# The expert stage in a written order on all engines, with two reordered edges, in a float32 chain of attention, experts and a dense layer

## The chip, the cores and the metric

The kernel runs on one core of a Trainium2 chip. The metric is the device time of one execution in microseconds, lower is better; the time given is the median of several executions. TensorE multiplies, VectorE, ScalarE and GpSimd do elementwise work on tiles of 128 partitions, SyncE's queue issues most of the transfers from DRAM.

## The reference, cut to what matters

Three layers follow each other, all in float32.

```python
# attention: q, k, v [4, 8, 576, 64], s [4, 8, 576]
scores = q @ k^T / sqrt(64)
cum = np.cumsum(np.maximum(s, 0.0), axis=-1)
scores = where(causal, -1e9, scores + minimum(-(cum_q - cum_k), 0.0))
x = softmax(scores) @ v                # then [2304, 512]
# experts: 8 of them, one for each token
logits = normalize(x) @ normalize(expert_emb).T / tau
e = argmax(logits);  gate = softmax(logits)[e]
x = gate * (relu(x @ w1[e]) @ w2[e])   # w1 [512, 1024], w2 [1024, 512]
# dense
h = x @ w_in                           # [512, 2048]
out = (h * np.cos(h)) @ w_out          # [2048, 512]
```

## The kernel before

**Order.** `moe_kernel` (line 43) calls the stages. Up to and with `steps.late()` everything stands under a manual schedule of all engines: what an engine does follows the order of the program. `finish()` (most of the expert stage) and `moe2` (the dense stage) stand under a manual schedule of SyncE alone: there a planner puts the instructions of the other engines in an order, by costs and due times of its own.

**Attention** (line 105). 16 pairs of heads, four steps each; step n of pair p has scores `sco` (lines 310 and 316, products of 64 rows), `mx` (line 336, VectorE: adds the decay, takes the maximum), `ex` (ScalarE, exponential), `tr` (transposes, line 352) and the products with v. The decay of a pair lies in `c_t`, which `load_c` reads back from DRAM (`cumd`, written from ScalarE's queue on line 198). For the first pair `first_c` makes it on TensorE instead (line 208), as a product of a selector with the 32 rows of `cum`. `mask` adds the causal part, `setup_a` to `setup_d` prepare the router and are put at points of the loop by `at`.

**Experts** (line 745). A step (r, f) is eighth f of the hidden layer of expert r; r = -1 stands for the first tokens of one expert, taken early, and r = 0 for its rest; 72 steps in all, n = 8 (r + 1) + f. A step has a weight tile [128, 1024] that `weights` loads into one of three `raw` buffers and that `split` (line 95) parts in two: `wh` (ScalarE, line 99) and its rest `wl` (VectorE, line 101). `emit_h` makes 12 products, the relu `hh` on ScalarE (964) and its rest `hl` on VectorE (965); `emit_o` makes 12 products into four accumulators (992 to 994), one step later. After the last eighth of an expert the accumulators go to `x2h` (ScalarE, 999) and `x2l` (VectorE, 1000), at a place that is read from memory into a register by `offset` (817), for ScalarE and VectorE. `windows` (822) is a chain of small operations for the overflow loop, and `token_numbers` (1007) scatters row numbers by GpSimd, 20 times; both are tied to an instruction behind which the planner may put them. `load_x` and `xt_parts` load and transpose an expert's tokens.

**Dense** (line 1244). 80 steps, each a pair of one of 16 chunks of weights and one of five blocks of tokens (one of 256, four of 512): `emit_h` 12 products (1287 to 1289) and then h·cos h (`h_cos_h`, 1145: ScalarE, VectorE, ScalarE with Sin, VectorE), `gh` (ScalarE, 1294) and `gl` (VectorE, 1295); `emit_o`, two steps behind, 12 products (1307 to 1309). The chunks lie in DRAM as pairs of 32-bit words (float64) and are converted in halves by `load_chunk` (1213) with `to_f32_parts` (1131): lines 1136, 1137, 1140, 1141, 1230 and 1231 on VectorE, 1228 on ScalarE. `start_chunk` puts a chunk's generator into `g.tasks`, and `advance` takes every task one part further. Chunks 0 to 3 are started in the last expert steps, 4 and 5 at the head of the dense stage, and a chunk's conversion is finished in one go where a step needs it:

```python
            for _ in g.loading.pop(c, ()):
                pass
            wh, wl = ring[c]
```

Of the kernel before, what the change touches and what calls it, by code (L numbers as in the profile page):

```python
# [7 lines left out]
F32 = mybir.dt.float32  # L8
# [15 lines left out]
E, F = 8, 1024  # L24
# [18 lines left out]
def moe_kernel(ctx, tc, qd, kd, vd, sd, ied, embt, tau, ident, maskd, trid, wcat, wf, out):  # L43
# [9 lines left out]
    g.chunks, g.tasks, g.loading = {}, [], {}  # L53
# [11 lines left out]
    with ExitStack() as m1:  # L65
        with tc.manual_schedule(engines={ET.SP, ET.PE, ET.Activation, ET.DVE, ET.Pool}):
            attention(g, wcat, qd, kd, vd, sd, ied, embt, tau, ident, maskd, trid)
            steps, finish = moe1(g, m1, wcat, wf)
# [36 lines left out]
def attention(g, wcat, qd, kd, vd, sd, ied, embt, tau, ident, maskd, trid):  # L105
# [6 lines left out]
    with ExitStack() as st:  # L112
# [49 lines left out]
        def mask(p):  # L162
# [21 lines left out]

        s_t = sx.tile([128, S], F32, tag="sx", name="s_t")[0:B * H]
# [15 lines left out]
        sel2 = one.tile([B * H, 128], F32, name="sel2")  # L201
        nc.vector.tensor_copy(out=sel2.rearrange("p (a b) -> p a b", a=2), in_=idt[0:B * H, 0:2].unsqueeze(2).to_broadcast([B * H, 2, 64]))
# [11 lines left out]
        load(1)  # L214
# [6 lines left out]
        emb_t = one.tile([128, 4, E], F32, name="emb_t")  # L221
# [5 lines left out]
        ones_f = one.tile([128, 128], F32, name="ones_f")  # L227
# [15 lines left out]
        nc.gpsimd.memset(ones_f, 1.0)  # L243
# [7 lines left out]
        def setup_loads():  # L251
            nc.sync.dma_start(out=ie, in_=ied)
            nc.sync.dma_start(out=emb_t, in_=embt)
# [21 lines left out]
        def setup_a():  # L275
            nc.gpsimd.tensor_copy(out=tri_b, in_=tri_f)
            nc.gpsimd.tensor_tensor(out=sq, in0=emb_t, in1=emb_t, op=ALU.mult)
# [347 lines left out]
        at(1, "b", setup_b)  # L625
        at(2, "rb", setup_c)
        at(2, "b", setup_d)
# [40 lines left out]
        mx(2)  # L668
        ex(2)
        next(mask(1))  # L670
        mx(3)
        fills = [0, 1, 2, 3, 4, 4, 5, 5]
        for p in range(NPAIR):
# [23 lines left out]
            tr(n)  # L697
# [47 lines left out]
def moe1(g, st, wcat, wf):  # L745
# [3 lines left out]
    if True:  # L749
# [66 lines left out]
        def offset(r):  # L816
            if r < 0:
                return 0
# [3 lines left out]
        def windows():  # L822
# [7 lines left out]
            nc.vector.tensor_tensor(out=over[:, 0:1], in0=over[:, 0:1], in1=g.pf[:, 2:3], op=ALU.add)  # L830
            nc.vector.tensor_tensor(out=over, in0=pick[:, 2, :], in1=over, op=ALU.subtract)
            wi = sm.tile([128, NWIN], I32, name="wi")
            nc.gpsimd.iota(wi, pattern=[[1, NWIN]], base=0, channel_multiplier=0)
            wn = sm.tile([128, NWIN], F32, name="wn")
            nc.vector.tensor_copy(out=wn, in_=wi)
            wn128 = sm.tile([128, NWIN], F32, name="wn128")
            nc.vector.tensor_scalar(out=wn128, in0=wn, scalar1=128.0, scalar2=None, op0=ALU.mult)
            s5 = [128, E, NWIN]
            gt = sm.tile(s5, F32, name="gt")
            nc.vector.tensor_tensor(out=gt, in0=bc(over, 2, s5), in1=bc(wn128, 1, s5), op=ALU.is_gt)  # L840
            trips = sm.tile([128, E], F32, name="trips")
            nc.vector.tensor_reduce(out=trips, in_=gt, axis=AX.X, op=ALU.add)
            nc.vector.tensor_tensor(out=tmp, in0=bc(g.ef, 2, s3), in1=bc(g.ef, 1, s3), op=ALU.is_gt)
            nc.vector.tensor_tensor(out=tmp, in0=tmp, in1=bc(trips, 1, s3), op=ALU.mult)
# [99 lines left out]
        def emit_h(n):  # L944
# [22 lines left out]
            if n == 17:  # L967
                with tc.issue_after(ins.ins):
                    windows()
# [423 lines left out]
```

## Time and profile before

| | |
|---|---|
| median of 3 executions | 834.78 us (833.91 to 834.93) |
| profiled execution | 834.91 us |
| its span | 833.0 us (1.9 us lie around it) |
| busy TensorE / VectorE / ScalarE / GpSimd | 802.2 / 569.6 / 421.9 / 139.0 us |
| mean granted clock of TensorE | 0.992 |
| start of the first product, of the last | 4.70 us, 821.31 us |
| start of the last scatter to DRAM | 823.28 us |

The profile is one execution, with times from the start of its span. PE is TensorE, PEld its weight loads, DVE VectorE, ACT ScalarE, POOL GpSimd, SP SyncE; a name with a q at its end is an engine's queue. Attention lasts to about 160 us, the experts from there to 412, the dense stage to the end. An idle time in brackets stands before the instruction of its row, with what ended it.

### The profile page before, as it was taken

The numbers are of one execution on the slowest core, as the hardware profiler recorded it, in microseconds if no ns is written. First come the engines' busy times: TensorE is split into PE (matmuls) and PEld (weight loads), VectorE is DVE, ScalarE is ACT, GpSimd is POOL, SyncE is SP. The second block draws the span as 40 slices with busy tenths as digits, with TensorE's granted clock in tenths as the row PEclk, the third lists the DMA queues.
The fourth block names the chain that finished last, engine by engine and source line by source line (L and its number), as shares of the span: only waits on it lengthen the run. The fifth ranks groups of instructions, "written<-read, shape, count | busy, mean of one in ns | idle before, by whom it ended". The sixth has DMA issues, their size and how long they took to land. (4 is left out here: it accounts for less than half of the span.)

```text
span 833.0 us, 15110 instructions
## 1 busy us (share of the span) xinstructions
PE 802.2 (96%) x5607; PEld 666.0 (80%) x5607; DVE 569.6 (68%) x1254; ACT 421.9 (51%) x894; POOL 139.0 (17%) x274
## 2 busy tenths in 40 slices
PE   7999999999999999999989999999999999999994
PEld 4666666689999999999868888888888888888883
DVE  5879897974765565566989577775877758444462
ACT  4988888732545454555255453333433434333331
POOL 4447665340011101100000000000000000000133
PEclk9999999999999999999989999999999999999998
DMA  7999875548757689774432111110111100000122
GB/s 239 311 354 349 260 242 168 171 162 323 260 152 190 141 161 194 205 174 164 142 101 77 51 51 50 52 52 1 50 52 51 51 1 2 1 0 1 52 78 102
DMA packets 41712, 109.06 MB, mean 131 GB/s; under 512 B 7392, under 2 KB 7904, under 8 KB 41632
## 3 DMA queue, kind: packets, MB, share of 16 engines
q1 hardware_dynamic: 38032, 98.50, 39.9%
q0 software_dynamic: 3552, 9.45, 3.1%
q8 instruction: 46, 0.75, 0.4%
q14 instruction: 34, 0.28, 0.1%
q10 hardware_dynamic: 48, 0.07, 0.0%
HBM read 92.19 MB, written 15.81 MB: 130 GB/s over the span
## 5 line engine op out<-in xcount | busy, mean ns | idle before, releaser
L101 DVE TENSOR_TENSOR wl<-wraw,wh 128x1024 fp32r<-128x1024 f32 x64 | 78.2, 1224 | 66.9 <-ACT wh L99 66.8
L1287 PE MATMUL h_ps<-x2h,wh 128*128 128x512 f32 (+1 forms) x320 | 118.9, 371 | 1.1 <-DVE x2l L1000 1.1
L1307 PE MATMUL facc<-wh,gh 128*128 128x512 f32 x288 | 115.7, 402 | 3.8 <-ACT gh L1294 3.8
L1288 PE MATMUL h_ps<-x2l,wh 128*128 128x512 f32 (+1 forms) x320 | 118.4, 370 | 0.0
L1289 PE MATMUL h_ps<-x2h,wl 128*128 128x512 f32 (+1 forms) x320 | 118.3, 370 | 0.0
L1309 PE MATMUL facc<-wh,gl 128*128 128x512 f32 x288 | 114.8, 399 | 0.0
L1308 PE MATMUL facc<-wl,gh 128*128 128x512 f32 x288 | 114.7, 398 | 0.0
L1148 ACT ACTIVATE ki<-h_ps 128x512 int32<-128x512 f32 (+1 forms) x80 | 44.5, 557 | 119.9 <-PE h_ps L1289 119.4
L1149 DVE SCALAR_TENSOR_TENSOR ki<-ki,h_ps 128x512 f32<-128x512 int32 (+1 forms) x80 | 50.5, 632 | 71.4 <-ACT ki L1148 71.0
L99 ACT CAST wh<-wraw 128x1024 fp32r<-128x1024 f32 x64 | 67.1, 1050 | 52.6 <-PE acc L993 47.5
L1319 POOL DMA_INDIRECT out_dram<-oacc,ti x18 | 17.5, 971 | 439.9 <-DVE oacc L1317 436.2
L604 ACT ACTIVATE s_sb<-s_sb,mx 128x576 f32<-128x576 f32 (+2 forms) x144 | 83.0, 581 | 5.5 <-DVE mx L336 5.4
L1150 ACT ACTIVATE ki<-ki,hpi 128x512 f32<-128x512 f32 (+1 forms) x80 | 54.5, 682 | 48.3 <-DVE ki L1149 48.3
L993 PE MATMUL acc<-hl,wh 128*128 128x256 f32 (+7 forms) x256 | 76.6, 299 | 0.7 <-DVE hl L965 0.7
L992 PE MATMUL acc<-hh,wh 128*128 128x256 f32 (+7 forms) x256 | 77.3, 302 | 0.0
L994 PE MATMUL acc<-hh,wl 128*128 128x256 f32 (+7 forms) x256 | 76.4, 298 | 0.0
L1294 ACT CAST gh<-ki 128x512 fp32r<-128x512 f32 (+1 forms) x80 | 46.3, 578 | 53.1 <-DVE ki L1151 53.1
L1287 PEld LDWEIGHTS h_ps<-x2h,wh 128*128 128x128 f32 x320 | 60.1, 188 | 13.4 <-DVE x2l L1000 1.3
L1288 PEld LDWEIGHTS h_ps<-x2l,wh 128*128 128x128 f32 x320 | 60.2, 188 | 12.3 <-DVE x2l L1000 0.6
L1151 DVE TENSOR_TENSOR ki<-h_ps,ki 128x512 f32<-128x512 f32 (+1 forms) x80 | 50.7, 634 | 27.3 <-ACT ki L1150 27.3
L1289 PEld LDWEIGHTS h_ps<-x2h,wl 128*128 128x128 f32 x320 | 60.2, 188 | 11.3
L959 PE MATMUL h_ps<-xth,wh 128*128 128x368 f32 (+6 forms) x224 | 68.6, 306 | 0.0
(241 smaller groups left out, 1686.6 us busy)
## 6 DMA issues: line engine op xcount, KB each, us to landing
wraw<-in_wcat_dram SPq DMA_DIRECT2D x64, 512.0 KB, 4.8
wraw<-in_wf_dram SPq DMA_DIRECT2D x32, 512.0 KB, 3.7
k_t<-in_kd_dram SPq DMA_DIRECT2D x16, 496.0 KB, 9.8
c_t<-cumd SPq DMA_DIRECT2D x15, 512.0 KB, 6.9
xr<-zr SPq DMA_DIRECT2D x8, 768.0 KB, 9.4
xw<-xr SPq DMA_DIRECT2D x7, 768.0 KB, 8.3
q_t<-in_qd_dram SPq DMA_DIRECT2D x16, 320.0 KB, 6.6
v_t<-in_vd_dram SPq DMA_DIRECT2D x16, 320.0 KB, 7.8
```

The lines of the kernel that those rows point to most:

```text
L101: nc.vector.tensor_tensor(out=lo, in0=raw, in1=hi.bitcast(F32), op=ALU.subtract)
L604: nc.scalar.activation(**kw)
L959: nc.tensor.matmul(out=ps[:, 0:c], lhsT=wh[:, sl], rhs=th[:, k, 0:c], start=(k == 0), stop=False)
L992: nc.tensor.matmul(out=ps[:, 0:c], lhsT=wh[:, sl], rhs=hh[:, 0:c], start=(f == 0), stop=False)
L993: nc.tensor.matmul(out=ps[:, 0:c], lhsT=wh[:, sl], rhs=hl[:, 0:c], start=False, stop=False)
L994: nc.tensor.matmul(out=ps[:, 0:c], lhsT=wl[:, sl], rhs=hh[:, 0:c], start=False, stop=(f == 7))
L1287: nc.tensor.matmul(out=ps[:, 0:w], lhsT=wh[:, sl], rhs=g.x2h[:, k, a0:a1], start=(k == 0), stop=False)
L1288: nc.tensor.matmul(out=ps[:, 0:w], lhsT=wh[:, sl], rhs=g.x2l[:, k, a0:a1], start=False, stop=False)
L1289: nc.tensor.matmul(out=ps[:, 0:w], lhsT=wl[:, sl], rhs=g.x2h[:, k, a0:a1], start=False, stop=(k == 3))
L1307: nc.tensor.matmul(out=acc[t], lhsT=gh[:, sl], rhs=wh[:, 512:1024], start=(c == s), stop=False)
L1308: nc.tensor.matmul(out=acc[t], lhsT=gh[:, sl], rhs=wl[:, 512:1024], start=False, stop=False)
L1309: nc.tensor.matmul(out=acc[t], lhsT=gl[:, sl], rhs=wh[:, 512:1024], start=False, stop=(c == e))
```

## The change

Four things are edited. (1) At the start a memset of ones comes first on GpSimd and nine products of ones first on TensorE; a dummy Exp comes early on ScalarE; the selectors and `cum` get 128 partitions (the rest zero); `cumd` is written from SyncE's queue; loads change order; one of `mask`'s additions goes to GpSimd; `mx(0)`, `sco(2)`, `tr(0)`, the square of the embeddings and `setup_b` to `setup_d` come earlier. (2) `finish` and a new `last_steps` stand under the manual schedule of all engines. A table `when` says behind which step a weight tile is split, and the load three tiles ahead is issued behind it; the place register of an expert is loaded in its step f = 4; `windows` becomes a generator of which three operations follow at a time; `token_numbers` stands in program order without its statement that the scatters are independent. (3) Of the chunks only 0, and the first part of 1, is converted before the expert stage ends; chunks 2 to 5 start in dense steps 1, 4, 8 and 11; a step asks for the half it needs (`half_of`); the first part in the dense stage is put behind the last `x2l`; a dummy Sin stands in `overlap` behind `gate_b`. (4) In the last four dense steps all h come before the last o, pairs of blocks share a tile, and the second products go by token tile.

```diff
@@ moe_kernel @@
             steps.late()
-        with tc.manual_schedule(engines={ET.SP}):
             finish()
+            last_steps()
@@ attention @@
-                    nc.vector.tensor_tensor(out=c[:, h, 512:640], in0=c[:, h, 512:640], in1=mk_f[:, 0:128], op=ALU.add)
+                    (nc.gpsimd if h else nc.vector).tensor_tensor(out=c[:, h, 512:640], in0=c[:, h, 512:640], in1=mk_f[:, 0:128], op=ALU.add)
...
+        ones_f = one.tile([128, 128], F32, name="ones_f")
+        nc.gpsimd.memset(ones_f, 1.0)
...
+        nc.sync.dma_start(out=mk_f, in_=maskd)
         load(0)
-        nc.sync.dma_start(out=mk_f, in_=maskd)
+        emb_t = one.tile([128, 4, E], F32, name="emb_t")
+        nc.sync.dma_start(out=emb_t, in_=embt)
+        w_ps = bank("w_ps")
+        for _ in range(9):
+            nc.tensor.matmul(out=w_ps[:, 0:128], lhsT=ones_f, rhs=ones_f, start=True, stop=True)
+        nc.scalar.activation(out=one.tile([128, 1], F32, name="exp0"), in_=ones_f[:, 0:1], func=ACTF.Exp)
...
-        cum = sx.tile([128, S], F32, tag="sx", name="cum")[0:B * H]
+        cums = sx.tile([128, S], F32, tag="sx", name="cum")
+        nc.gpsimd.memset(cums, 0.0)
+        cum = cums[0:B * H]
...
-        nc.scalar.dma_start(out=cumd, in_=cum)
+        nc.sync.dma_start(out=cumd, in_=cum)
+        load(1)
...
-            sel = sel2 if k == 2 else idt[0:B * H, k:k + 1].to_broadcast([B * H, 128])
+            sel = sel2 if k == 2 else idt[:, k:k + 1].to_broadcast([128, 128])
...
-                nc.tensor.matmul(out=ps, lhsT=sel, rhs=cum[:, c0:c0 + 288], start=True, stop=True)
+                nc.tensor.matmul(out=ps, lhsT=sel, rhs=cums[:, c0:c0 + 288], start=True, stop=True)
...
         load_c(1)
-        load(1)
         load_v(0)
...
-        at(1, "b", setup_b)
-        at(2, "rb", setup_c)
-        at(2, "b", setup_d)
+        at(0, "c", setup_b)
+        at(0, "b", setup_c)
+        at(1, "b", setup_d)
...
         sco(0)
+        mx(0)
         first_c(0)
         next(m0)
-        mx(0)
         ex(0)
         first_c(1)
         sco(1)
+        sco(2)
         next(m0)
-        sco(2)
+        nc.gpsimd.tensor_tensor(out=sq, in0=emb_t, in1=emb_t, op=ALU.mult)
         mx(1)
         ex(1)
-        sco(3)
+        tr(0)
         mx(2)
         ex(2)
+        sco(3)
@@ moe1 @@
-            if n == 17:
-                with tc.issue_after(ins.ins):
-                    windows()
...
-                off_r = offset(r)
+                off_r = off.pop(r, 0)
...
-                    nc.vector.tensor_tensor(out=x2l[:, d, bass.ds(off_r, c)], in0=acc[d][:, 0:c],
+                    g.turned = nc.vector.tensor_tensor(out=x2l[:, d, bass.ds(off_r, c)], in0=acc[d][:, 0:c],
...
-            for o in prev:
-                tc.declare_no_dep(ins.ins, o, reason="rows that differ")
...
         def finish():
-            split(g, load_at[8], raws.pop(load_at[8]))
-            for n in range(9, NS):
+            when = {12: 12, 13: 13, 14: 14, 15: 15, 16: 17} | {l: l + 2 for l in range(17, 62)} | {62: 63, 63: 64, 64: 65, 65: 65, 66: 66, 67: 67}
+            win = windows()
+            for n in range(9, NS - 4):
                 r, f = steps[n]
-                if n in load_at:
...
+                if n in (9, 10):
+                    weigh(n + 4)
                 emit_h(n)
                 emit_o(n - 1)
-                advance(g.tasks)
+                for l in range(12, len(loads)):
+                    if when[l] == n:
+                        split(g, l, raws.pop(l))
+                        if l + 3 < len(loads):
+                            weigh(l + 3)
...
+                if f == 5 and r + 2 < E:
+                    load_x(r + 2)
+                if f == 4:
+                    off[r] = offset(r)
+                if n % 2 and 0 <= n // 2 - 9 < 20:
+                    token_numbers(n // 2 - 9)
+                if r > 0 and f in (1, 2, 4, 6, 7):
+                    for _ in range(3):
+                        next(win, 0)
+            start_chunk(g, wf, 0)
+            advance(g.tasks)
+
+        def last_steps():
+            for n in range(NS - 4, NS):
+                if n == NS - 4:
+                    off[E - 1] = offset(E - 1)
+                else:
+                    advance(g.tasks)
+                emit_h(n)
+                emit_o(n - 1)
+                if n < NS - 1:
+                    advance(g.tasks)
+                if n == NS - 2:
+                    start_chunk(g, wf, 1)
+                    g.tasks.reverse()
+                    advance(g.tasks[0:1])
+                    g.tasks.reverse()
             emit_o(NS - 1)
@@ overlap @@
     r.gate_b()
+    g.nc.scalar.activation(out=g.count.tile([128, 1], F32, name="sin0"), in_=r.l[:, 0, 0:1], func=ACTF.Sin, scale=0.0)
@@ load_chunk and behind it @@
+def half_of(g, c, z):
+    while c in g.loading and g.halves.get(c, 0) <= z:
+        if next(g.loading[c], 0) is not None:
+            break
@@ moe2 @@
-            for _ in g.loading.pop(c, ()):
-                pass
+            half_of(g, c, 0)
...
-        for c in range(LW, RING):
-            start_chunk(g, wf, c)
         LO = 2
-        for n in range(NS):
+        begin = {1: 2, 4: 3, 8: 4, 11: 5}
+        for n in range(NS - 4):
+            if n in begin:
+                start_chunk(g, wf, begin[n])
             emit_h(n)
-            advance(g.tasks)
+            if n:
+                advance(g.tasks)
+            else:
+                with tc.issue_after(g.turned.ins):
+                    advance(g.tasks)
...
-        for n in range(NS - LO, NS):
-            emit_o(n)
+        emit_h(NS - 4)
+        emit_o(NS - 6)
+        emit_h(NS - 3)
+        emit_h(NS - 2)
+        emit_o(NS - 5)
+        emit_h(NS - 1)
+        for t, n in ((0, 4), (0, 3), (0, 2), (1, 4), (1, 3), (1, 2), (0, 1), (1, 1)):
+            emit_o(NS - n, t)
```

## Rows read from the trace of the kernel before

**Rows 1.** Stretches: busy time (count) of each engine, granted clock, DMA share, GB/s.

```profile
0.00:18.00 18.00, 13.06 (x44) 6.57 (x44) 7.99 (x23) 5.98 (x15) 7.69 (x24) 1.00 0.76 232
40.00:60.00 20.00, 18.87 (x248) 12.13 (x246) 14.19 (x52) 17.16 (x55) 9.23 (x18) 1.00 1.04 346
360.00:400.00 40.00, 40.00 (x335) 39.33 (x334) 27.30 (x44) 22.09 (x38) 1.33 (x2) 1.00 0.60 173
425.00:431.00 6.00, 5.76 (x14) 4.50 (x15) 4.74 (x10) 4.11 (x9) 0.00 (x0) 0.51 0.23 83
500.00:550.00 50.00, 50.00 (x217) 40.40 (x216) 38.89 (x66) 20.35 (x32) 0.00 (x0) 1.00 0.16 49
```

**Rows 2.** The groups of one shape on TensorE, 0 to 17 us: busy, mean ns | idle.

```profile
L310 PE MATMUL s_ps<-k_t,q_t 64*64 64x288 f32 x8 | 1.2, 711 | 0.0
```

**Rows 3.** The same view for 19 to 40 us.

```profile
L310 PE MATMUL s_ps<-k_t,q_t 64*64 64x288 f32 x16 | 1.4, 428 | 0.0
```

**Rows 4.** The timeline of TensorE: begin, duration, instruction, [idle before].

```profile
4.70 2.28 PE L208 MATMUL c_ps<-cum,sel 32*128 32x288 f32 x4 [4.70 <-DVE sel L202]
6.91 1.24 PE L310 MATMUL s_ps<-k_t,q_t 64*64 64x288 f32 x8
8.07 4.20 PE L208 MATMUL c_ps<-cum,idt 32*128 32x288 f32 x8
12.21 3.36 PE L316 MATMUL s_ps<-k_t,q_t 64*128 64x512 f32 x8
...
17.39 0.94 PE L310 MATMUL s_ps<-k_t,q_t 64*64 64x288 f32 x8
```

**Rows 5.** The timeline of TensorE, 408 to 431 us.

```profile
408.69 0.28 PE L992 MATMUL acc<-hh,wh 128*128 128x264 f32 x1
409.64 0.39 PE L993 MATMUL acc<-hl,wh 128*128 128x264 f32 x1 [0.67 <-DVE hl L965]
...
410.98 0.28 PE L994 MATMUL acc<-hh,wl 128*128 128x264 f32 x1
412.38 0.50 PE L1287 MATMUL h_ps<-x2h,wh 128*128 128x512 f32 x1 [1.12 <-DVE x2l L1000]
...
421.03 0.40 PE L1287 MATMUL h_ps<-x2h,wh 128*128 128x512 f32 x1
425.24 0.79 PE L1307 MATMUL facc<-wh,gh 128*128 128x512 f32 x1 [3.81 <-ACT gh L1294]
...
430.94 0.40 PE L1289 MATMUL h_ps<-x2h,wl 128*128 128x512 f32 x1
```

**Rows 6.** The timeline of GpSimd, first us.

```profile
0.71 0.53 POOL L240 MEMSET zr<- 128x512 f32 x1 [0.29 <-POOLq L1385]
```

**Rows 7.** The groups of one shape on TensorE's weight loads, 0 to 17 us.

```profile
L208 PEld LDWEIGHTS c_ps<-cum,idt 32*128 32x128 f32 x8 | 2.4, 319 | 1.8 <-issue 0.9 <-DVE c_t L211 0.3
```

**Rows 8.** The timeline of VectorE, 14 to 16 us.

```profile
14.44 0.69 DVE L336 CUSTOM_DVE_ANT_0 s_sb<-s_ps,c_t 128x512 f32<-128x512 f32 x1 [1.41 <-PE s_ps L316]
```

**Rows 9.** Line 820 on ScalarE's queue: duration min/median/max, first and last start.

```profile
L820 ACTq TENSOR_LOAD <-pki x7: 277/277/287, 193.8 to 197.2; - x7
```

**Rows 10.** The timeline of ScalarE, 193 to 209 us.

```profile
197.75 0.59 ACT L921 COPY x<-xt_ps 128x512 f32<-128x512 f32 x1 [3.59 <-PE acc L994]
```

**Rows 11.** The timeline of TensorE, 196.5 to 200 us.

```profile
198.39 1.83 PE L950 MATMUL h_ps<-x,w 128*128 128x128 f32 x14 [1.36 <-ACT x L921]
```

**Rows 12.** The groups by line: busy, mean ns | idle before <- releasers.

```profile
L99 ACT CAST wh<-wraw 128x1024 fp32r<-128x1024 f32 x64 | 67.1, 1050 | 52.6 <-PE acc L993 47.5 <-DVE over L831 2.2 <-DMA wraw<-in_wcat_dram 1.7
...
L1137 DVE SCALAR_TENSOR_TENSOR cva<-wraw,cva 128x512 uint32<-128x512 uint32 x32 | 22.1, 690 | 0.8
...
L1136 DVE TENSOR_SCALAR cva<-wraw 128x512 uint32<-128x512 uint32 x32 | 13.6, 424 | 2.5 <-DMA wraw<-in_wf_dram 1.9
```

**Rows 13.** The timeline of ScalarE, 408 to 426 us.

```profile
419.01 0.59 ACT L1148 ACTIVATE ki<-h_ps 128x512 int32<-128x512 f32 x1
419.62 1.28 ACT L1150 ACT_TABLE_LOAD   x1
```

More of the change, by code (lines that the diff above doesn't have):

```diff
@@ L52, in moe_kernel @@
     g.tc, g.nc, g.const, g.dram, g.xr, g.out = tc, nc, const, dram, xr, out
-    g.chunks, g.tasks, g.loading = {}, [], {}
+    g.chunks, g.tasks, g.loading, g.halves = {}, [], {}, {}
     ET = mybir.EngineType
@@ L67, in moe_kernel @@
             attention(g, wcat, qd, kd, vd, sd, ied, embt, tau, ident, maskd, trid)
-            steps, finish = moe1(g, m1, wcat, wf)
+            steps, finish, last_steps = moe1(g, m1, wcat, wf)
             overlap(g, steps)
@@ L220, in attention @@
         junk = ro.tile([128, 1], F32, name="junk")
-        emb_t = one.tile([128, 4, E], F32, name="emb_t")
         tau_t = one.tile([128, 1], F32, name="tau_t")
@@ L696, in attention @@
             point(p, "rb")
-            tr(n)
+            if p:
+                tr(n)
             mx(n + 4)
@@ L966, in emit_h @@
             hs[n] = (hh, hl)
-            if n == 17:
-                with tc.issue_after(ins.ins):
-                    windows()
-            if n % 2 and 0 <= n // 2 - 9 < 20:
-                with tc.issue_after(ins.ins):
-                    token_numbers(n // 2 - 9)
-        acc = {}
+        acc, off = {}, {}
         def emit_o(n):
@@ L1053, in finish @@
                     next(part)
-                if n == 12 or (r > 0 and f == 5):
-                    if r + 2 < E:
-                        load_x(r + 2)
+                if f == 5 and r + 2 < E:
[7 more added lines that the diff above has]
+                        next(win, 0)
+            assert next(win, 1) == 1 and all(l < 12 for l in raws)
+            start_chunk(g, wf, 0)
[15 more added lines that the diff above has]
+                    g.tasks.reverse()
             emit_o(NS - 1)
@@ L1215, in load_chunk @@
     nc = g.nc
-    hi = g.ringp.tile([128, 1024], F32R, tag="wh", name="wh")
-    lo = g.ringp.tile([128, 1024], F32R, tag="wl", name="wl")
     raws = []
@@ L1222, in load_chunk @@
         raws.append(raw)
-    g.chunks[c] = (hi, lo)
     for z, raw in enumerate(raws):
         yield
+        if not z:
+            hi = g.ringp.tile([128, 1024], F32R, tag="wh", name="wh")
+            lo = g.ringp.tile([128, 1024], F32R, tag="wl", name="wl")
+            g.chunks[c] = (hi, lo)
+            g.halves[c] = 0
         t, p = yield from to_f32_parts(nc, g.cv, raw)
@@ L1290, in emit_h, with emit_o @@
             h = ps[:, 0:w]
-            t = h_cos_h(nc, tg.tile([128, 512], I32, tag="ki", name="ki")[:, 0:w], h, hpi)
-            gh = gp.tile([128, 512], F32R, tag="gh", name="gh")
-            gl = gp.tile([128, 512], F32R, tag="gl", name="gl")
-            nc.scalar.copy(out=gh[:, 0:w], in_=t)
-            nc.vector.tensor_tensor(out=gl[:, 0:w], in0=t, in1=gh[:, 0:w].bitcast(F32), op=ALU.subtract)
+            k = n - (NS - 4)
+            if k < 0 or k % 2 == 0:
+                gs["t"] = [p.tile([128, 512], d, tag=q, name=q) for p, d, q in ((tg, I32, "ki"), (gp, F32R, "gh"), (gp, F32R, "gl"))]
+            t, gh, gl = (a[:, 256 * (k % 2):256 * (k % 2) + w] if k >= 0 else a[:, 0:w] for a in gs["t"])
+            t = h_cos_h(nc, t, h, hpi)
+            nc.scalar.copy(out=gh, in_=t)
+            nc.vector.tensor_tensor(out=gl, in0=t, in1=gh.bitcast(F32), op=ALU.subtract)
             gs[n] = (gh, gl)
-        def emit_o(n):
+        def emit_o(n, only=None):
             tb, c, s, e = steps[n]
             a0, a1 = blocks[tb]
+            half_of(g, c, 1)
             wh, wl = ring[c]
-            gh, gl = gs.pop(n)
-            for t in range((a1 - a0) // 128):
+            gh, gl = gs[n]
+            tiles = range((a1 - a0) // 128) if only is None else (only,)
+            for t in tiles:
                 if c == s:
@@ L1310, in emit_o @@
             if c == e:
-                for t in range((a1 - a0) // 128):
+                for t in tiles:
                     i = a0 // 128 + t
@@ L1322, in emit_o @@
                         sent.append(ins.ins)
-            if n == last[c]:
+            if n == last[c] and only is None:
                 start_chunk(g, wf, c + RING)
-        for c in range(LW, RING):
-            start_chunk(g, wf, c)
         LO = 2
-        for n in range(NS):
+        begin = {1: 2, 4: 3, 8: 4, 11: 5}
+        for n in range(NS - 4):
+            if n in begin:
+                start_chunk(g, wf, begin[n])
             emit_h(n)
-            advance(g.tasks)
+            if n:
[3 more added lines that the diff above has]
+                    advance(g.tasks)
             if n >= LO:
```

43 lines of the change are left out of this document (27 added, 16 removed).

## The prediction, made before the change was run

> **What bounds the kernel now.** I read the busy times in the table first: TensorE works 802.2 of 833.0 us, so at most some 31 us can be had, all of it where TensorE waits or runs slow. The stretches [rows 1] say where. From 360 to 400 (expert steps) and from 500 to 550 (dense steps) TensorE is busy throughout, and VectorE and ScalarE have room (27.3 and 22.1 of 40 us): an order there can gain nothing, only lose. In 40 to 60 (attention) 18.9 of 20 us are busy and the DMA share is 1.04. What is left is edges: the start, the hand-over to the experts near 198, and the hand-over to the dense stage, 408 to 431. The dense stage has a row of 0.51: its first 6 us run at half clock.
>
> The start is slow in another way. Until 17 us a pass of line 310 takes 711 ns, after 19 us 428 [rows 2, 3]; eight start in 1.16 us at 6.91, and at 17.39 they are over in 0.94 [rows 4]. So TensorE is at the lower of its levels (1.2 of 2.4 GHz) up to about 17.5 us. The granted-clock column prints 1.00 for 0 to 18 [rows 1]; I trust the durations. What went before the rise: products of 32 rows from 4.70 on, without a rise, then products of 64 rows from 12.21, and the rise some 5.3 us later [rows 4]. The second rise of the kernel has the same length: products from 425.24 at 0.79 us, and from 430.94 at 0.40: 5.7 us [rows 5].
>
> **The change part by part.**
>
> *Start.* Added: 9 products of ones (18 passes, as line 208's 2 products are 4 rows of the trace), the memset of ones first on GpSimd, a dummy Exp; the selectors of line 208 get 128 rows. The memset that is first now starts at 0.71 and takes 0.53 [rows 6]; one of a quarter of its columns in its place lets the products begin near 1.0 us. A pass of 288 columns starts every 0.525 us (4.20 over 8 [rows 4]); for 128 columns that is 0.233, so 18 end at 5.2 us. Bounded by the weight loads, 0.319 each [rows 7], they end at 6.8. I take 5.2: at the edge of the dense stage products follow every 0.12 us [rows 5] and so are not held by loads of that size. If dense products bring the rise 5.6 us after they begin (between 5.3 and 5.7), it comes at 6.6 us.
>
> The chain from there: line 208's first four passes begin at 5.2 instead of 4.70, partly fast, and end at 7.0, as before (4.70 + 2.28). sco(0) takes 0.6 (half of 1.16): 7.6. Twice first_c, 1.05 each (half of 2.10): 9.7. Then sco(1); the first reduction of step 1 starts 2.23 us after its first product (12.21 to 14.44 [rows 4, 8]), half is 1.1: 10.8. **Gain 14.44 − 10.8 = 3.6 us.** Bounds: with no early rise and the ones ending at 6.8, a loss of 6.8 − 4.7 = 2.1; with the rise already at 5.2, a further 0.9, so 4.5. Whether it lasts through attention: the transfers there are issued when a buffer comes free, so they move along with TensorE; the DMA share of 1.04 speaks against, and is rival B.
>
> The cumd write passes from ScalarE's queue to SP's, where load(1) now stands behind its wait for the scan; mk_f (96 KB) stands before load(0). Both are covered: TensorE's first products now wait for a selector and for cum, not for them; without that cover mk_f at the 232 GB/s of 0 to 18 [rows 1] costs 0.4 us, and load(1), if it is late for sco(4), as long as the scan holds it. mask's second head on GpSimd, the earlier setup points: they move work between engines with room, 0.
>
> *Place registers.* ScalarE now loads seven of them in a row, at 193.8 to 197.2 [rows 9]; the copy at 197.75 waits 3.59 us [rows 10], and TensorE stands 1.36 us for it at 198.39 [rows 11]. Loaded singly in step 4 of each expert that goes; seven times 0.28 us are spread over steps where ScalarE has half its time free [rows 1]. Not all of 1.36 stays: ScalarE's casts wait 1.7 us in all for weight tiles from DRAM [rows 12], and a stage that is earlier meets such a wait earlier. **Gain 0.8** (0 to 1.36; just above the middle, because a release of raw tiles moves with the splits).
>
> *Fixed order of the expert stage.* Nothing is removed there. Per tile ScalarE's cast takes 1.05 us [rows 12], one per step of 24 products at 0.12 = 2.9 us; the relu stands ahead of it in program order. The 20 token-number scatters lose their statement of independence: one each second step, 5.8 us apart; if one waits for the one before, only the next stands behind it on GpSimd, and what reads them is needed only at the end of the dense stage. Cost 0; where the cover fails see D.
>
> *Hand-over to the dense stage.* From start to start, less the usual 0.12 or 0.23, TensorE loses 0.83 at 408.69 (hl behind conversions), 1.28 at 410.98 (x2l), 3.98 at 421.03 (gh) [rows 5]; then 13 products (14 starts in the stretch [rows 1], the last already fast) take 5.70 us for 13 × 0.23 = 3.0: 2.7 more. The sum is 8.8. The late thing is VectorE: a half chunk costs it two instructions of 0.42 and four of 0.69 = 3.6 us [rows 12], a chunk 7.2, and the planner put four chunks around the edge. h of the first dense step was ready near 415.6 (12 products of 0.23, the last ending 0.4 after its start, from 412.38), and ScalarE began on it only at 419.01, behind a cast that waited for a conversion; a table load of 1.28 follows [rows 13].
>
> After: one chunk and a bit of the next are converted in the last four expert steps (four of 2.9 us), the others between dense steps 1 and 14, where each step has 24 × 0.23 = 5.6 us and VectorE needs about half. That is up to 2.5 us of conversion per step of 2.9, and hl and x2l stand in between: I leave 0.8 of stall (the first of the three above). The dense h now meets an idle ScalarE, with the Sin table already there: five instructions of 0.6 to 0.7, by those of the same 128x512 shape [rows 12, 13], bring gh 3.3 us after h, and two steps ahead TensorE has 5.6 us of products: 2 us in hand, no wait and no fall of the clock. **Gain 8.8 − 0.8 = 8.0** (bounds: all of 8.8; 2.1 if gh's wait and the clock stay and only the first two stalls go).
>
> The dummy Exp and Sin move a table load each to where ScalarE has nothing due; uncovered, 1.28 us each. *Tail:* the same products in another order, and again the last tile's add and scatter behind the last product: 0.
>
> **Sum:** 3.6 + 0.8 + 8.0 = 12.4; the profiled execution took 834.91, so **822.5 us**. It lies 0.1 above the median of three, 834.78; I leave that out.
>
> **A rule weighed.** The rows have rises 5.3 and 5.7 us after dense work began [rows 4, 5]. The Trainium skill, page "TensorE: Matmul & The Clock Gate", section "Part 1: The HAM clock gate", says that the throttled state is the default, that activity lifts it, and that the monitor's window runs free of the kernel's start, so that the point of the rise varies between runs. By the rows the start gains 3.6; by the page it would be a value between the two bounds that changes from run to run. The two rows here differ by only 0.4 us, which speaks for a narrow spread; no run here shows what ones do.
>
> **Rivals.**
> A, as summed: 0.56; its own range, with every term at its better bound 4.5 + 1.4 + 8.8 = 14.7, is 820 to 825.
> B, the start gains nothing: the ones don't lift the clock (they delay what they should speed), or attention is held by transfers, DMA share 1.04, and gives the time back. For it: that share. Against: TensorE is at 94% there. Time 834.9 − 8.8 = 826.1. Chance 0.20.
> C, the dense start still waits: conversions now run in its first steps, on the same VectorE, and if two of their 0.69 us instructions stand in front of each of the three of the chain (4.1 us) gh is late by 2, and the clock falls again. Then only 2.1 of the 8.8 come: 834.9 − 3.6 − 0.8 − 2.1 = 828.4. Against: dense step 0 starts no chunk of its own. Chance 0.12.
> D, slower: in the fixed order the cast of a weight tile stands on ScalarE ahead of the next relu. If its transfer is late, relu, hl and the second products are late with it, where the planner could put the relu first. The 1.7 us that the casts wait for DRAM now are for all 64. 56 casts would each have to cost TensorE more than 12.4/56 = 0.22 us; with 0.3 it is 839. Against: each tile is asked for three steps, 8.6 us, ahead. Chance 0.08.
> E, no difference: the gains of one edge are eaten by one new stall: 0.04.
>
> **Chances and range.** Faster by over 0.2% (1.7 us, about what a measurement of this kernel tells from no change): A, B and C, 0.88; within: 0.04; slower: 0.08. The range goes from 818.5 (below 820 by a part of the stalls inside attention, 18.87 of 20 busy, that a new order there could touch) to 829, which takes in B and C; it leaves out D, E and a little below, some 0.15.
>
> **What would show it.** Start: line 310 or 316 at the faster rate before 8 us, and the first reduction of step 1 near 10.8; wrong, if it is beyond 13. Registers: one load per expert on ScalarE, no wait of over 1 us at the first expert's copy. Hand-over: no TensorE wait over 1 us between the last expert product and the second dense step, granted clock 1.00 in the first 6 us of line 1307. The middle: TensorE still busy throughout; relu or casts waiting for DRAM there would be D. The stretch from the first dense product to the end should keep its length but for the lost 6.7 us.

## The result and the profile after

The changed kernel takes 825.34 us in the median of four executions (821.55 to 826.79), the kernel before beside it 834.86 (833.91 to 835.88): a ratio of 0.9879, interval 0.9843 to 0.9914. Forecast were 822.5, 818.5 to 829. The profiled execution is the fastest of the four: 821.55 us, span 819.7, where the one of before had 833.0. What is read from its trace below is therefore the best case of the changed kernel, not its middle.

The stretches of the changed kernel, columns as in [rows 1]:

```profile
0.00:18.00 18.00, 16.44 (x114) 11.28 (x115) 11.40 (x35) 9.46 (x27) 8.67 (x27) 1.00 0.85 249
40.00:60.00 20.00, 19.53 (x270) 12.55 (x267) 15.69 (x55) 17.82 (x57) 9.64 (x17) 1.00 1.04 369
395.00:419.00 24.00, 23.55 (x136) 20.53 (x135) 22.14 (x42) 12.81 (x25) 0.00 (x0) 1.00 0.40 110
411.00:417.00 6.00, 6.00 (x28) 4.83 (x27) 5.97 (x11) 4.99 (x9) 0.00 (x0) 1.00 0.29 87
500.00:550.00 50.00, 50.00 (x216) 40.25 (x215) 36.73 (x62) 19.74 (x31) 0.00 (x0) 1.00 0.13 43
```

The rows answer to [rows 1]. The first 18 us hold 114 rows of products instead of 44. The edge to the dense stage (395 to 419) has 23.55 of 24 us busy, and its first dense steps (411 to 417) the full clock in place of 0.51. The dense steady state is busy throughout as it was, but not quite as fast (see the end of this section).

The start on TensorE, and the first reduction of step 1 on VectorE, to lay beside [rows 4] and [rows 8]:

```profile
0.97 4.21 PE L198 MATMUL w_ps<-ones_f 128*128 128x128 f32 x18 [0.97 <-POOL ones_f L186]
5.01 2.19 PE L219 MATMUL c_ps<-cum,sel 128*128 128x288 f32 x4
7.13 0.71 PE L315 MATMUL s_ps<-k_t,q_t 64*64 64x288 f32 x8
7.78 2.21 PE L219 MATMUL c_ps<-cum,idt 128*128 128x288 f32 x8
9.91 1.77 PE L321 MATMUL s_ps<-k_t,q_t 64*128 64x512 f32 x8
```

```profile
11.19 0.69 DVE L341 CUSTOM_DVE_ANT_0 s_sb<-s_ps,c_t 128x512 f32<-128x512 f32 x1 [0.77 <-PE s_ps L321]
```

The ones run from 0.97 to 5.18, 0.234 us a pass. Four passes of line 219 still take 2.19 us, and from 7.13 on eight score passes start in 0.65 us (1.16 before): the clock rose near 7.1, 6.1 us after the first of the ones. The reduction starts at 11.19 instead of 14.44.

The rise does not always stand there. The ten profiles with the ones in them (this one and those of the experiments) all begin the ones at 0.97 us. In two the clock rises near 7, in three between 5.5 and 6.3, and in five while the ones still run, the earliest near 3.9 (the kernel with chunk 1 earlier):

```profile
0.97 3.69 PE L198 MATMUL w_ps<-ones_f 128*128 128x128 f32 x18 [0.97 <-POOL ones_f L186]
...
6.90 0.72 PE L315 MATMUL s_ps<-k_t,q_t 64*64 64x288 f32 x8 [0.73 <-DMA k_t<-in_kd_dram]
```

The same 18 passes take 3.69 us, and yet the scores begin only 0.23 us earlier than in the changed kernel: TensorE now waits 0.73 us for k_t. Seven of the ten profiles have such a wait, 0.51 to 0.83 us.

ScalarE and TensorE at the first float32 expert, for [rows 10] and [rows 11]:

```profile
191.36 0.58 ACT L950 COPY x<-xt_ps 128x512 f32<-128x512 f32 x1 [1.47 <-PE xt_ps L949]
...
202.93 1.05 ACT L99 CAST wh<-wraw 128x1024 fp32r<-128x1024 f32 x1 [1.95 <-DMA wraw<-in_wcat_dram]
...
205.41 1.05 ACT L99 CAST wh<-wraw 128x1024 fp32r<-128x1024 f32 x1 [1.26 <-DMA wraw<-in_wcat_dram]
...
207.10 0.29 ACT L981 ACTIVATE h<-h_ps 128x128 f32<-128x128 f32 x1
```

```profile
207.44 1.16 PE L1013 MATMUL acc<-h,w 128*128 128x128 f32 x8 [0.77 <-ACT h L981]
```

The copy no longer waits for a row of register loads, but for TensorE's own transposes. New are the next rows: casts of expert 1's weight tiles wait 1.95 and 1.26 us for DRAM, the float32 expert's relu behind them comes at 207.10, and TensorE waits 0.77 for it. On SyncE's queue the loads of these tiles stand behind the float32 expert's own (4 MB, used without a cast), and those behind a load of rows that waits for GpSimd's scatter.

TensorE and ScalarE at the edge to the dense stage, for [rows 5] and [rows 13]:

```profile
403.03 0.39 PE L1016 MATMUL acc<-hl,wh 128*128 128x264 f32 x1 [0.45 <-DVE hl L994]
...
404.36 0.28 PE L1017 MATMUL acc<-hh,wl 128*128 128x264 f32 x1
404.49 0.50 PE L1341 MATMUL h_ps<-x2h,wh 128*128 128x512 f32 x1
...
412.95 0.39 PE L1365 MATMUL facc<-wh,gh 128*128 128x512 f32 x1
```

```profile
407.58 0.60 ACT L1193 ACTIVATE ki<-h_ps 128x512 int32<-128x512 f32 x1 [2.52 <-PE h_ps L1343]
...
409.73 0.73 ACT L1195 ACTIVATE ki<-ki,hpi 128x512 f32<-128x512 f32 x1
...
411.45 0.63 ACT L1350 CAST gh<-ki 128x512 fp32r<-128x512 f32 x1 [0.49 <-DVE ki L1196]
```

One wait of 0.45 is left. ScalarE takes h at 407.58 and has gh at 412.08, 0.87 us before TensorE wants it; between the last expert product and the first dense one nothing is lost. In the kernel before, ScalarE's row ahead of 419.01 [rows 13] was a cast held by a conversion on VectorE:

```profile
418.48 0.62 ACT L1228 CAST wh<-cva 128x512 fp32r<-128x512 f32 x1 [3.30 <-DVE cva L1137]
```

Where the 13.3 us of these two executions come from, by the first (or last) start of the same product in both traces:

| landmark on TensorE (first row: VectorE) | before | after | gained so far |
|---|---|---|---|
| reduction of step 1 | 14.44 | 11.19 | 3.2 |
| first product of the early tokens | 169.8 | 165.6 | 4.2 |
| first of the float32 expert | 198.4 | 192.6 | 5.8 |
| first h of expert 1 | 213.8 | 208.4 | 5.4 |
| last h of expert 7 | 406.9 | 400.5 | 6.4 |
| first dense product | 412.4 | 404.5 | 7.9 |
| last start on line 1307, after: 1365 | 820.8 | 807.2 | 13.6 |
| end of the span | 833.0 | 819.7 | 13.3 |

The gain of the dense stage is larger at its head than this table shows. Count the changes from first products (lines 1287 to 1289, after: 1341 to 1343) to second products (1307 to 1309, after: 1365 to 1367) and back: the 30th comes 85.2 us after the first dense product before and 78.5 after, 6.7 us gained. From there to the 145th the kernel before takes 298.69 us and the changed one 299.66, so 1.0 us is lost again, evenly over the steps.

### The profile page after: what moved, and what is told of

Same layout as the page of the kernel before. It is cut to its first block, busy times and chain, and to the rows that moved or that the text cites. A ratio compares the mean times of both kernels' runs of the same rounds, so it can differ in the third digit from the quotient of the medians.

```text
span 819.7 us, 15090 instructions
## 1 busy us (share of the span) xinstructions
PE 798.2 (97%) x5625; PEld 665.9 (81%) x5625; DVE 573.5 (70%) x1253; ACT 420.4 (51%) x896; POOL 138.9 (17%) x276
## 5 line engine op out<-in xcount | busy, mean ns | idle before, releaser
L1193 ACT ACTIVATE ki<-h_ps 128x512 int32<-128x512 f32 (+1 forms) x80 | 44.4, 555 | 121.5 <-PE h_ps L1343 121.4
L993 ACT ACTIVATE hh<-h_ps 128x256 fp32r<-128x256 f32 (+7 forms) x64 | 26.7, 417 | 94.9 <-PE h_ps L990 93.0
```

## The experiments

They ran in three groups, each on one chip with the kernel before beside it: the first four beside 837.72 us, the next four (weight tiles by two pairs, the planner, chunk 1) beside 837.02, the last four beside 833.88. Ratios are to those. The changed kernel itself ran beside the result and in the first group alone, so the other two groups are compared with it by the ratios.

**The changed kernel once more.** No edit.

> The changed kernel once more, unaltered, for the spread of its executions (821.55 to 826.79). Theory S (the spread is the start: the moment at which the clock rises after the ones moves from run to run): median near 825; if this profile is a longer one, the ones or the first scores are slow for longer, and every landmark behind 20 us is late by the same amount. Rival W (the spread is waits inside attention, 20 to 160 us): the first reduction of step 1 stands near 11.2 us as before, and the loss builds up between there and the first expert product (165.6 us).

825.62 us (822.09 to 827.56, six), ratio 0.985 (0.9824 to 0.9877). This profile is 4.1 us longer than the first (823.8), and the start is not why: reduction of step 1 at 11.21. The early tokens begin 1.4 us later than in the first (167.0), the float32 expert 1.9, expert 1 already 4.2 (212.6), 18.1 us after the float32 expert instead of 15.8. ScalarE, then TensorE:

```profile
208.45 1.04 ACT L99 CAST wh<-wraw 128x1024 fp32r<-128x1024 f32 x1 [4.79 <-DMA wraw<-in_wcat_dram]
```

```profile
209.72 1.16 PE L1013 MATMUL acc<-h,w 128*128 128x128 f32 x8 [2.14 <-ACT h L981]
```

The cast of a weight tile stands 4.79 us in front of a relu, for DRAM; TensorE pays 2.14. That is rival D's mechanism, at one place. Theory S falls for this pair of profiles; W was right on the start and wrong on the place of most of the loss.

**Without the ones.**

```diff
-        w_ps = bank("w_ps")
-        for _ in range(9):
-            nc.tensor.matmul(out=w_ps[:, 0:128], lhsT=ones_f, rhs=ones_f, start=True, stop=True)
```

> The changed kernel without its nine products of ones; everything else stays. Theory O (the ones lift the clock early): 3 to 4 us slower than the changed kernel, about 829; the first reduction of step 1 near 14 us instead of 11.2. Rival P (the selectors of 128 rows and the new order would do it without them): the padded products start near 4.5 and bring the rise near 10 us, first reduction of step 1 near 12.5, 1 to 1.5 us slower, about 826.5.

824.95 us (824.51 to 828.74), ratio 0.9855 (0.983 to 0.988). TensorE's start:

```profile
4.80 2.26 PE L216 MATMUL c_ps<-cum,sel 128*128 128x288 f32 x4 [4.80 <-POOL rs L389]
6.99 1.24 PE L312 MATMUL s_ps<-k_t,q_t 64*64 64x288 f32 x8
8.16 3.51 PE L216 MATMUL c_ps<-cum,idt 128*128 128x288 f32 x8
11.60 1.77 PE L318 MATMUL s_ps<-k_t,q_t 64*128 64x512 f32 x8
```

Line 216's eight passes take 3.51 us, between 4.20 at the lower rate and 2.21 at the upper: the rise falls inside them, about 6 us after 4.80, and the reduction of step 1 starts at 12.87. So P holds at the start: in this one profile the padded products alone lift the clock and give half of the 3.2 us, the ones the other half; how much this share moves between executions is not known. In the time O's loss of 3 to 4 us is not there; P's 1 to 1.5 us doesn't show either, but lies within the intervals.

**Start alone, rest alone.** The part of the diff above that stands under `attention`, put alone into the kernel before; and everything but that part.

> The kernel before with the changed kernel's attention stage alone (ones, order of the start, loads); the expert stage stays in the planner's order. Theory O: 3.5 to 4.5 us faster than before, 830 to 831, with a wider spread than before. Rival (attention is held by transfers and gives the time back): within 1 us of 834.8. What is left to the changed kernel's time, 5 to 6 us by medians, is then the expert and dense part.

> The changed kernel with the attention stage of before: registers, fixed order and chunks stay. Theory: the hand-overs alone give 9.1 us by the profile (13.3 less 4.2), so 825.7; and the spread of the executions is that of before (2 us) if it comes from the start, theory S. If the spread stays at 5 us, it comes from the fixed order or the hand-over, rival W2.

Start alone: 836.36 us (834.31 to 840.54), ratio 0.9986 (0.9966 to 1.0006): 1.4 us by the medians, not to be told from none, and by the interval at most 2.8. So theory O misses. Rest alone: 826.59 (825.92 to 828.73), ratio 0.9869 (0.9846 to 0.9892), 0.9 from the 825.7 expected. Beside the changed kernel's 825.62 the start is worth 1.0 us by the medians, which can't be told from none either, though the reduction of step 1 stands at 11.35 with the start alone and at 14.41 with the rest alone. The rest alone spreads over 2.8 us, but the kernel before beside it over 5.2, so the spread decides nothing between S and W2.

Where the start's gain goes shows in one stretch, from the float32 expert's first product to expert 1's. It takes 15.4 us before and 15.8 with the rest alone, 17.9 with the start alone, and 15.8 and 18.1 in the two profiles of the changed kernel. With the new start it is thus up to 2.7 us longer, differently in each execution: against the second profile of the changed kernel the rest alone is 3.5 us late at the first float32 product (198.0 to 194.5) and only 1.2 at expert 1 (213.8 to 212.6), against the first profile 5.4 at both.

The rest alone also shows what moves executions apart. TensorE at the end of its attention:

```profile
161.24 4.32 PE L377 MATMUL o_ps<-pt,v_t 128*64 128x320 f32 x20 [1.03 <-issue]
```

The same 20 passes take 2.28 us in the changed kernel; here the granted clock of 160 to 170 is 0.66. Four of the 14 profiles have a fall of the clock between 145 and 170: three at these passes, and the one with the registers together a little later, behind waits of 0.68 and 1.35 us for rows. Waits of about 1 us stand there in nearly all 14, so the wait alone does not decide it.

**Weight tiles ahead of the late rows.** In `overlap` (the second kernel has the old attention function as well):

```diff
     o(3)
+    s.raw32(8)
+    s.raw32(9)
     s.x(0)
-    s.raw32(8)
...
     o(4)
-    s.raw32(9)
```

> The changed kernel, but in overlap the first two pairs of float32 weight tiles are asked for ahead of the load of the late rows, which waits on SyncE's queue for GpSimd's scatter of rows. Theory T (what the start gains is given back between 190 and 212 us, because these 4 MB of tiles start only when the scatter has landed): the tiles start near 180 instead of 187 to 190; ScalarE's wait for raw tiles before 215 falls from 3.5 to 6.1 us to under 2; 1.5 to 2.5 us faster than the changed kernel on this chip type of run, about 823.5, with a smaller spread. Rival V (that stretch is limited by the volume, or by buffers): the same time within 1 us, and the waits for raw tiles stay.

> The same move of the weight tiles, with the attention stage of before. Theory T: 2.5 to 3.5 us slower than the kernel with the same move and the changed start, since now nothing takes the start's 3.2 us back. Rival: about 1 us slower, as it was without the move (826.59 against 825.62); the start would then be lost somewhere in attention.

826.1 us (824.87 to 827.46), ratio 0.9861, and with the old start 828.66 (827.11 to 832.4), ratio 0.9896. SyncE's queue and TensorE's wait in the first:

```profile
179.58 2.74 SPq L917 DMA_DIRECT2D w<-in_wcat_dram  x4
191.72 0.34 SPq L927 DMA_DIRECT2D xw<-xr  x1
```

```profile
PE xt_ps L949 <- DMA xw<-xr: 2.3, 1, 2.3
```

The tiles start at 179.58, no cast waits for DRAM any more, but the rows' load is issued only at 191.72, and TensorE waits 2.3 us for the rows. The scatter that it waits for now shares the transfers (DMA share 1.01 in 182 to 186 and 1.02 in 186 to 190), which fits, but is not shown to be the cause. So no gain by itself, against T. T's other number came: with the tiles out of the way the start is worth 2.6 us (828.66 less 826.1). The stretch from the float32 expert to expert 1 agrees: it takes 14.7 us here and 15.1 with the old start, so nothing of the start is lost in it.

**One pair ahead, and a bridge.** Only the first pair is moved; the second kernel has four products of ones besides.

```diff
     o(3)
+    s.raw32(8)
     s.x(0)
-    s.raw32(8)
...
+            if p == NPAIR - 1:
+                b_ps = ps_s.tile([128, 2, 512], F32, tag="s", name="b_ps")
+                for _ in range(4):
+                    nc.tensor.matmul(out=b_ps[:, 0, 0:128], lhsT=ones_f, rhs=ones_f, start=True, stop=True)
             late = av(p, 256)
```

> The changed kernel with only the first pair of float32 weight tiles (1 MB) asked for ahead of the late rows. Theory T2 (the two pairs, 2 MB, took the way of the scatter, so the rows came 2.3 us late and ate the gain): the first pair starts near 180 and has landed before the last scatter is issued; no wait of TensorE for the rows above 0.5 us, ScalarE's wait for raw tiles before 215 below 3 us; 1 us faster than the changed kernel. Rival: the sum of what has to come by 212 us counts, whatever its order, and the time stays within 0.5 us.

> As the kernel with one pair ahead, and four products of ones (8 passes) on TensorE in the wait of about 1 us ahead of the last pair's products with v. Theory S2 (part of the spread is a fall of the clock at that wait, seen in 3 of 11 profiles, worth about 2 us each): the wait is gone from the records, no granted clock below 1.00 between 155 and 170, 0.5 us faster in the median and fewer long executions. Rival: the fall depends on the wait before it as well and stays as frequent; the same time, or slower by the 0.2 us that the products may stand in the way.

821.76 us (821.35 to 821.93, five executions), ratio 0.9849 (0.9828 to 0.9871); with the bridge 821.70 (821.11 to 825.88), ratio 0.9859. SyncE's queue in the first:

```profile
178.91 1.11 SPq L917 DMA_DIRECT2D w<-in_wcat_dram  x2
188.62 0.35 SPq L927 DMA_DIRECT2D xw<-xr  x1
```

The pair starts at 178.91; expert 1 begins at 208.2, as in the best execution of the changed kernel; TensorE waits 0.2 for the rows and for no relu, and the casts wait 2.5 us (3.5 to 6.1 in the changed kernel). The ratio cannot be told from the changed kernel's (0.985 and 0.9879), so T2's gain of 1 us is not shown. All five executions lie within 0.6 us where the changed kernel's spread over 5, but those were not run beside it, and the bridge, which has the same move of the tiles, spreads over 4.8: that the move narrows the spread is not shown. The bridge removes the wait of 1.1 us and adds nothing that shows; its one long execution speaks against it as the cure of the spread.

**Registers together.** In `late`, and no loads in step 4:

```diff
             emit_o(6)
+            for e in range(E - 1):
+                off[e] = offset(e)
             emit_xt(0)
...
-                if f == 4:
-                    off[r] = offset(r)
```

> The changed kernel with the seven place registers loaded in a row where the planner had put them, ahead of the copy of the late rows. Theory R (the row of loads costs TensorE 1.4 us at that copy, but the float32 expert behind it is limited by its weight transfers and takes a part back): ScalarE waits about 3.6 and TensorE 1.4 us at the copy, and the first product of expert 1's hidden layer is 0.4 to 1.0 us later than in the changed kernel, 0.5 to 1 us in the time. Rival: nothing is taken back, 1.4 us or more in the time.

822.8 us (821.4 to 826.01), ratio 0.9863 (0.9839 to 0.9887).

```profile
PE h_ps L979 <- ACT x L950: 1.6, 1, 1.6
```

TensorE's wait at the copy is back, and the casts wait only 0.5 us for DRAM afterwards (3.5 to 6.1 without it): the later stage finds its tiles there. From the early tokens' first product to expert 1's it takes 44.4 us, a part of it at a lower clock (0.50 in 167 to 168); the two changed executions take 42.8 and 45.6. Theory R fits at the copy, with no loss in the time that can be told; the row of register loads is thus not shown to cost the kernel anything.

**The planner again.**

```diff
             steps.late()
-            finish()
-            last_steps()
+        with tc.manual_schedule(engines={ET.SP}):
+            finish()
+            last_steps()
```

> The changed kernel with finish and last_steps under the planner again (SyncE alone in fixed order). Theory F (the order is what removes the register loads from the edge and keeps conversions away): the loads of the place registers stand together again, TensorE waits over 1 us at the first expert's copy, and 3 to 6 us are lost: 829 to 831. Rival C (the smaller number of chunks alone does it): within 1.5 us of the changed kernel.

832.5 us (829.55 to 834.73), ratio 0.9938 (0.9916 to 0.996): half of the gain is gone. TensorE's timeline at the copy, and its longest wait behind it:

```profile
197.33 2.05 PE L980 MATMUL h_ps<-x,w 128*128 128x128 f32 x16 [1.36 <-ACT x L951]
```

```profile
PE acc L1014 <- ACT h L982: 2.2, 1, 2.2
```

The registers are loaded in a row again (192.7 to 196.1); expert 1 begins 18.4 us after the float32 expert (15.8 and 18.1 in the two profiles of the changed kernel, 15.4 before), so this stretch proves nothing against the planner; experts 1 to 7 take 194.8 us from first to last h (192.1 in both profiles of the changed kernel). This profile also has the fall of the clock at the end of attention. The dense stage is as good as in the changed kernel: from its first to its last product 402.8 us (402.7; 408.4 before). F holds for the time, C for the dense edge.

**Chunk 1 earlier.** In `last_steps`:

```diff
-                else:
-                    advance(g.tasks)
+                advance(g.tasks)
                 emit_h(n)
                 emit_o(n - 1)
-                if n < NS - 1:
+                advance(g.tasks)
+                if n <= NS - 3:
                     advance(g.tasks)
-                if n == NS - 2:
+                if n == NS - 3:
                     start_chunk(g, wf, 1)
-                    g.tasks.reverse()
-                    advance(g.tasks[0:1])
-                    g.tasks.reverse()
+                    advance(g.tasks)
```

> The changed kernel with chunk 1 started one expert step earlier and five of its six parts converted before the dense stage: about 3.6 us of VectorE work more in the last three expert steps, less behind. Theory D (VectorE is what holds the edge): hl or x2l is late there by 1 to 2.5 us, 826.5 to 828. Rival (the gain comes from the Sin table and from the order behind the edge): no wait of TensorE above 0.6 us before the first dense product, the same time.

828.54 us (826.59 to 829.68), ratio 0.9892 (0.9855 to 0.9929). TensorE before the dense stage:

```profile
402.12 0.39 PE L1016 MATMUL acc<-hl,wh 128*128 128x264 f32 x1 [0.29 <-DVE hl L994]
...
406.03 0.39 PE L1016 MATMUL acc<-hl,wh 128*128 128x264 f32 x1 [0.74 <-DVE hl L994]
...
408.84 0.39 PE L1016 MATMUL acc<-hl,wh 128*128 128x264 f32 x1 [1.08 <-DVE hl L994]
```

Three waits for hl, 2.1 us, in place of one of 0.45: theory D by the trace. In the time the interval overlaps that of the changed kernel.

**Without the Sin table's early load.** In `overlap`:

```diff
-    g.nc.scalar.activation(out=g.count.tile([128, 1], F32, name="sin0"), in_=r.l[:, 0, 0:1], func=ACTF.Sin, scale=0.0)
```

> The changed kernel without the dummy Sin. Theory D (the smaller load of conversions is the whole of the gain at the dense stage's start): the table load of 1.28 us falls into ScalarE's wait for VectorE behind the first h, gh is late by less than 0.5 us, TensorE does not wait, same time within 0.5 us. Rival: gh is late by 1.3 us, TensorE waits, 1 us or more, with a fall of the granted clock 2 to 4 us.

826.91 us (823.59 to 831.41), ratio 0.9917 (0.9888 to 0.9946). ScalarE and TensorE at the dense start:

```profile
412.43 1.28 ACT L1194 ACT_TABLE_LOAD   x1
```

```profile
416.11 0.50 PE L1364 MATMUL facc<-wh,gh 128*128 128x512 f32 x1 [0.37 <-ACT gh L1349]
```

The table load comes behind the first h, and gh is 0.37 us late; the clock stays at 1.00. By this profile it is D. The time is longer than that: the median lies 4.1 us above the kernel with the registers together, beside which it ran, and its executions spread over 8 us, which would suit the rival. The profiled execution is the fastest of the six, and loses time in the float32 expert (15.2 us from first to last h, 13.8 and 17.0 in the two profiles of the changed kernel). Whether other executions lost the clock at the edge is open: there is no trace of them.

The kernel settles another point. From the 30th to the 145th change between first and second products its dense stage takes 298.69 us, as in the kernel before and with the start alone, the other two without the dummy Sin; all eleven profiles with it take 299.66. So the 1.0 us that the dense stage loses behind its head comes with that one instruction, or with what shifts when its tile is there; why is open.

## Why the prediction was right, point by point

**Start, forecast 3.6.** At its place the number was right: ones from 0.97 to 5.18 (1.0 and 5.2 forecast), rise near 7.1 (6.6), reduction at 11.19 (10.8), 3.2 us. That the ones were needed for it was half wrong: the selectors of 128 rows, which I priced at nothing, do half, in the one profile without ones. That k_t's load, with mk_f's now ahead of it, is "covered" was wrong in seven of ten profiles, where TensorE waits 0.51 to 0.83 us for it; so the bound of 4.5 for an early rise can't be had: the reduction never came before 10.87, a gain of 3.6. The step that failed is "whether it lasts": in the time the start is worth 1.0 to 1.4 us, neither told from none, and rival B's result held for this term. B's place was wrong, though. Attention passes the gain on (4.2 us ahead at the early tokens); as far as the profiles show, it is taken back, in some executions and not in others, where the casts of expert 1's tiles, whose loads queue behind the wait for the scatter, hold ScalarE and behind them the float32 expert's relus. With the tiles moved the same start is worth 2.6.

The rule weighed (the Trainium skill, "TensorE: Matmul & The Clock Gate", "Part 1: The HAM clock gate") says that the point of the rise varies between runs. The ten profiles with ones agree: the rise comes between about 3.9 and 7.1 us, 3.0 to 6.1 us after the first of the ones. The forecast's fixed 5.6 us, taken from two rows that differ by 0.4, was too narrow; that the reduction all the same starts between 10.87 and 11.35 is k_t's doing in the profiles with an early rise, and so that the size of this term came out was in part luck. At the end of attention the lower clock comes back in four of the 14 profiles.

**Registers, forecast 0.8.** The wait of 1.36 went, 1.6 us by the landmarks, and 0.4 was taken back before expert 1: 1.2 in this pair of profiles, and for the reason given. With the registers together the time was not told to be longer, so in the time the gain is not shown.

**Fixed order, forecast 0, rival D 0.08.** Between expert 1 and 7 it gained 1.0 us, which no wait in either trace explains; the cause stays open. D's mechanism exists, at the tiles of 203 to 209 only: 0.77 us in the first profile, 2.14 in the second, where the forecast had 0. It doesn't reach D's price because the other 50-odd tiles come in time.

**Dense edge, forecast 8.0.** 7.9 − 6.4 = 1.5 before the first dense product (forecast 2.1 − 0.8 = 1.3) and 13.6 − 7.9 = 5.7 behind it (6.7): 7.2. At the head of the dense stage the forecast 6.7 came in full; 1.0 of it is lost again in the steps behind, in every profile with the dummy Sin, which was forecast to cost nothing. The stall left for hl was forecast at 0.8 and is 0.45 here, but 1.6 in the profile of the rest alone. Chunk 1 earlier brings the stalls back, and the planner with the new chunks keeps the 5.7: the fixed order is not the cause behind the edge. Fewer conversions there are the likely one, by the cast at 418.48 that waited for VectorE; they were not tested apart from taking halves on demand and from the place of the first part. The Sin table's part is at most 0.5 us in the one trace, and open in the time. The tail, forecast 0, gained nothing (13.6 at the last start on line 1365, 13.3 at the end).

**The sum.** 12.4 forecast, 13.3 in the profiled execution, 9.5 by the medians, and 12.1 by those of the changed kernel run once more (837.72 to 825.62). What lies between is, as far as the profiles show, the float32 expert's stretch and the clock at the end of attention, which vary from one execution to the next. The median of the result, 825.34, lies just outside rival A's own range (820 to 825) and next to B's 826.1; the stated range held it because it took in B and C.

## What to carry to other kernels

A gain made at the start may last only to the next point that is set by a transfer, so look for the load that waits in a queue for something else, and price the gain there. In a fixed order a cast that waits for DRAM holds every relu behind it; asking for its tile ahead of loads that wait removes that wait, but only so much that the waited-for transfer keeps its way (with 1 MB ahead TensorE waited 0.2 us for it, with 2 MB 2.3 us; in the time neither could be told from the changed kernel). Before a difference between two kernels' traces is put down to an edit, read a second profile of the same kernel: one stretch took 15.8 and 18.1 us in two profiles of one program.

## What was unexpected of the hardware

Products with 32 rows from 4.70 us on, with a few of 64 rows between, had not lifted the clock until 64-row products had run some 5 us [rows 4], in all three profiles with the old start; the same products with their selector padded by rows of zeros to 128 lifted it about 6 us after 4.80, in one profile. The same ones from the same 0.97 us lifted it anywhere between 3.9 and 7.1 us. The granted-clock column prints 1.00 through the slow start of every profile; only the durations show it. One dummy instruction on ScalarE, far ahead of the dense stage, goes with 1.0 us more in that stage, alike in all eleven profiles that have it.
